# The add passes over VectorE's exponential tiles moved to GpSimd, with other planner quotas

## The chip, the cores and the metric

The kernel runs on one core of a Trainium2 chip. The metric is the device time of one execution in microseconds. Times before: 855.03 and 853.03 us in two runs, median 854.03.

## The reference

The output mixes two branches of one sequence `x` (2048 x 512) with a gate per row. Branch a is full softmax attention with 32 heads of 16 columns, branch b is a convolution whose kernel comes from a diagonal state-space model with 128 states per channel.

```python
x = A_x
g = _sigmoid((x * gate_w).sum(-1, keepdims=True))
a = _A_ref(x, A_wqkv, A_wo)          # scores = q k^T / 4, softmax, times v, times wo
b = _B_ref(x, B_A_re, B_A_im, B_B_re, B_B_im, B_C_re, B_C_im, B_log_dt, B_Dskip)
return g * a + (1 - g) * b
```

## The kernel before

**Attention.** The scores of a block (512 queries of 4 heads) against 128 keys and one head are a tile of 128 x 512. There are 2048 such tiles; three of them make a group, and there are 683 groups, the last of two tiles. TensorE writes a group's scores into one of two PSUM buffers `SC0`, `SC1` (`qk`), then the exponential is taken, and TensorE multiplies the result with the values and adds it up in `OA` (`pv`). As there are two score buffers, the scores of group g+2 cannot be written before group g is read.

**Two engines for the exponential.** ScalarE takes the exponential of a whole group in one instruction (`ex`, line 913, tiles `ET`). In some groups it takes only two of the three tiles and VectorE takes the third (`bits`, line 949): a multiplication and an addition, written as a 16-bit integer, give the bit pattern of a bf16 number near the exponential (tile `DZ`). Four such groups in a row make a set, that is four tiles of the same 128 keys, one for each of the four heads, 128 x 2048 together. To come nearer to the exponential, `batch` adds two constants to the bit patterns (`step`, line 960): 42 gives `DU`, and later 84 gives a new `DZ` in place. TensorE multiplies `DZ`, `DU` and the second `DZ` with the values (`VE`) and with scaled copies of them (`VS`) and adds all three products in `OA`, where the scale corrects each pattern's share. A set thus has four evictions from PSUM, two add passes of 128 x 2048 and 12 products for 4 tiles. Sets have buffers by window of groups: two in groups 180 to 400, two in 400 to 640, three in 640 to 678.

**The other branch.** Beside the attention run the projections, the parameters of the state-space model (VectorE), a table `PT` of powers by block of 32 channels (VectorE, written to `gm_ptd`), from it the states by chunk (`sstage`: TensorE, eviction to `SG`), two scans over 32 chunks (`scan`, half of the channels each, 30 steps of four VectorE operations between two SBUF tensors, lines 1333 to 1340; GpSimd issues one DMA per step, line 1342, out of four buffers `G`), and then 32 y units (`ystage`). Units 0 to 15 need the first scan, 16 to 31 the second. A unit loads `Py` and four pieces of `Tt` (SP's queue, three buffers each), multiplies into the PSUM buffer `MB`, which one user at a time can hold, is evicted as `Yst` (line 1414) and written to DRAM; two units later make a block that SP reads back transposed as `Yl`. When all 16 blocks are back, VectorE adds `Yl` to the attention output of the first three quarters (`AR`), SP loads `Wo`, and TensorE, VectorE and ScalarE finish the last quarter.

**What sets the order.** The program is recorded by a planner (`Sched`) before it runs: each engine gets its instructions in one fixed order, and each waits for what it needs. The planner books a cost for every instruction and takes what its clock says is ready. `decide` chooses the groups of which VectorE takes a tile: a new set begins when VectorE's idle time that is not used up reaches a quota (`dvq`, table `DVQ`, by which stage is already done: `scan1` is the second scan, `scan0` the first, `S15` the last block of states). Idle time saved up is cut at `DVCAP`.

```python
def dvq():
    return next(n for f, n in DVQ if f is None or f in sch.flag)
...
    plan["used"] = max(plan["used"], idle() - DVCAP)
    if plan["set"] is None and clear(x) and idle() - plan["used"] >= dvq():
```

Of the kernel before, what the change touches and what calls it, by code (L numbers as in the profile page):

```python
# [11 lines left out]
ALU = mybir.AluOpType  # L12
# [37 lines left out]
VSP = [len(k) * VSW for k in VKT]  # L50
VSAT = (168, 600)
WIN = ((180, 400, 2, 1), (400, 640, 2, 1), (640, 678, 3, 2))
DVQ = (("scan1", 0.2), ("scan0", 0.8), ("S15", 2.0), (None, 0.7))
BP = 2.2
DVCAP = 2.0
BUP = 1
VW = 136
VG = 4 * VW + 16
# [31 lines left out]
class Prog:  # L90
# [5 lines left out]
    def __init__(self, bufs):  # L96
        self.bufs = bufs
        for b in bufs.values():
            b.st, b.tags, b.closed, b.first, b.last = {}, {}, False, None, None
        self.q = -1  # L100
        self.cap = None
        self.act = 0
        self.cfg = None
        self.busy = 0.0
        self.marg = {}
        self.log = []
        self.tm = {e: 0.0 for e in self.ENG}
        self.fin = {}
        self.ops = {e: [] for e in self.ENG}
        self.cnt = {e: 0 for e in self.ENG}  # L110
        self.known = {e: {} for e in self.ENG}
        self.snap = {}
        self.dn = [0] * (NDSEM + NPSEM)
        self.dnext = self.pnext = 0
        self.need = {e: set() for e in self.ENG}
# [82 lines left out]
    def op(self, eng, fn, R=(), W=(), c=.1, lat=.085, a=0, cfg=None):  # L198
        if self.cap is not None:
            self.cap.append((self.op, (eng, fn, R, W), dict(c=c, lat=lat, a=a, cfg=cfg)))  # L200
            return
        if cfg is not None:
            if cfg != self.cfg:
                c += TURN[cfg]
            self.cfg = cfg
        self.act += a
        self.log.append((self.op, self.q, (eng, fn, R, W)))
        deps = self._deps(eng, R, W)
        i = self.cnt[eng]
        at = self.tm[eng]  # L210
        for s, k in deps.items():
            at = max(at, self.fin[(s, k)] + (.03 if s == eng else .05))
        self.tm[eng] = at + c
        if eng == "DVE":
            self.busy += c
        self.fin[(eng, i)] = at + c + lat
        self.cnt[eng] += 1
        self._record(eng, fn, deps, eng, i, R, W)
        return at + c + lat

    def dma(self, eng, fn, R=(), W=(), c=.45, lat=3.0, m=DMARG):
        if self.cap is not None:
# [393 lines left out]
def record(nc, p, B, ins):  # L616
# [6 lines left out]
    op, dma = p.op, p.dma  # L623
# [331 lines left out]
    def batch(i):  # L955
        z, u, q, b = (sets[i][x] for x in ("z", "u", "q", "b"))
        R = [(z, k, (i, k)) for k in range(4)]

        def step(t, k, W):
            op("DVE", lambda v: v.tensor_scalar(t.u16(0, [[1, 2048]]), z.u16(0, [[1, 2048]]), float(STEP[k][0]), None, ALU.add), R, W, c=.07 + 2048 / 3840)  # L960

        def terms(t, k):
            for n, j in enumerate(sets[i]["js"]):
                pv_mm(4 * q + j, t, 512 * n, [(u, 0, i) if t is u else (z, n, (i, n) if k is None else (i, n, "t"))], QUAD if n == 0 else 0, k)

        yield ("DVE", .6, BUP)
        step(u, 0, [(u, 0, i)])
        yield ("AFTER", f"pv{16 * b}")
        if i:
            yield ("AFTER", f"dvp{i - 1}")  # L970
        yield ("PE", QUAD)
        terms(z, None)
        yield ("AFTER", f"VS{int(q % 16 not in VKT[0])}")
        yield ("PE", QUAD)
        terms(u, 0)
        yield ("DVE", .6, BUP)
        step(z, 1, [(z, k, (i, k, "t")) for k in range(4)])
        yield ("PE", QUAD)
        terms(z, 1)
        sch.mark(f"dvp{i}")  # L980
# [799 lines left out]
```

## Time and profile before

| what | us |
|---|---|
| median of two runs | 854.03 |
| span of the profiled execution | 854.3 |
| ScalarE busy | 826.1 |
| VectorE busy | 766.1 |
| TensorE busy (modelled ends) | 756.7 |
| GpSimd busy | 44.0 |

The profiled execution's own time is its span from the first to the last instruction, 854.3 us, 0.3 above the median of the runs. Busy times of the engines lie beside each other; a row of the group view gives busy time, the mean duration of one, and the idle time ahead of the group with what ended it. Durations of neighbouring instructions on one engine overlap, so that spacing is a better price than the mean duration. In the profile `PE` is TensorE's matmul, `PEld` its weight load, `DVE` VectorE, `ACT` ScalarE, `POOL` GpSimd and `SP` the engine that issues most DMAs; a `q` behind an engine's name is its queue.

### The profile page before, as it was taken

The page shows a single profiled execution, that of the slowest core. Times are in us where ns is not written, and L with a number is a line of the kernel's source. Part 1 is how long each engine was busy: PE and PEld are TensorE (multiplying, and loading weights), DVE is VectorE, ACT ScalarE, POOL GpSimd, SP SyncE. Part 2 cuts the span into 40 slices and gives each one's busy share as a digit, 9 for nine tenths or more (in the row PEclk, how much of TensorE's full clock was granted, in tenths as well). Part 3 has the DMA queues.
Part 4 walks back from the last instruction along what each step waited for, and adds up shares of the span by engine and source line. Part 5 has one row for each costly group of instructions (what it writes and reads, how often), then busy time and mean ns, then how long its engine had stood idle before and what let it go on. Part 6 is the DMA issues. An engine that isn't in the chain of part 4 may idle for free.

```text
span 854.3 us, 23568 instructions
## 1 busy us (share of the span) xinstructions
PE 756.7 (89%) x10301; PEld 296.5 (35%) x10301; DVE 766.1 (90%) x1271; ACT 826.1 (97%) x695; POOL 44.0 (5%) x73
## 2 busy tenths in 40 slices
PE   7888888788768999999999899889988899999986
PEld 3232332222212434343443344334442234443321
DVE  5799999999969988898898999999999978997994
ACT  6999999999979999999999999999999999999996
POOL 4000000000000000000010111101111100000000
PEclk9999999999989999899998999999999999999999
DMA  9400102942933498477394597248998425645120
GB/s 206 118 2 10 35 3 82 194 153 81 73 129 152 51 206 103 149 131 164 62 162 71 84 192 116 36 104 166 199 191 151 120 88 121 136 120 113 25 99 26
DMA packets 218168, 94.55 MB, mean 111 GB/s; under 512 B 185168, under 2 KB 205008, under 8 KB 216016
## 3 DMA queue, kind: packets, MB, share of 16 engines
q1 hardware_dynamic: 207408, 83.99, 45.6%
q0 software_dynamic: 8640, 7.87, 5.9%
q8 instruction: 81, 1.33, 0.6%
q10 hardware_dynamic: 2016, 1.18, 0.6%
q14 instruction: 23, 0.19, 0.1%
HBM read 35.17 MB, written 30.82 MB: 77 GB/s over the span
## 4 chain that ended last, share of the span: by engine, by line
ACT 66%; PE 23%; DMA 5%; DVE 4%; SPq 1%; issue 0%; ACTq 0%; DVEq 0%
ACT ET L913 65%; PE OA L632 9%; PE SC L632 7%; PE MB L632 7%; DMA gm_gd<-g 3%; DMA gm_ytd<-Yst 1%; DMA gm_ptd<-PT 1%; DVE DZ L949 1%; DMA Wq<-in_A_wqkv_dram 1%; DVE s L1333 1%; DVE s L1335 1%; DVE G L1340 0%; DVE s L1338 0%; DVE tt L1007 0%; SPq L1488 0%
## 5 line engine op out<-in xcount | busy, mean ns | idle before, releaser
L913 ACT ACTIVATE ET<-SC 128x1536 bf16<-128x1536 f32 (+1 forms) x683 | 817.8, 1508 | 15.1 <-PE SC L632 13.9
L632 PE MATMUL SC<-Qm,KT 32*128 32x512 bf16 x2048 | 276.5, 387 | 75.9 <-ACT ET L913 61.1
L632 PE MATMUL OA<-wm 128*32 128x256 bf16 (+3 forms) x2193 | 251.6, 341 | 1.2 <-DVE wm L685 1.2
L632 PE MATMUL OA<-ET,VE 128*32 128x512 bf16 x1800 | 181.6, 395 | 4.6 <-DVE OT L984 4.4
L949 DVE TENSOR_SCALAR DZ<-SC 128x512 uint16<-128x512 f32 x248 | 166.2, 685 | 19.1 <-PE SC L632 16.8
L632 PEld LDWEIGHTS SC<-Qm,KT 32*128 32x128 bf16 x2048 | 70.7, 91 | 291.8 <-ACT ET L913 233.9
L632 PEld LDWEIGHTS OA<-wm 128*32 128x32 bf16 (+2 forms) x2193 | 72.9, 95 | 33.8 <-issue 15.5
L632 PEld LDWEIGHTS OA<-ET,VE 128*32 128x32 bf16 x1800 | 46.1, 93 | 106.1 <-issue 98.4
L632 PE MATMUL MB<-X,Qt 64*128 64x32 bf16 x1024 | 74.5, 231 | 0.0
L632 PEld LDWEIGHTS MB<-X,Qt 64*128 64x128 bf16 x1024 | 57.7, 109 | 25.2 <-issue 23.0
L1310 DVE TENSOR_SCALAR SG<-MB 128x512 bf16<-128x512 f32 x64 | 43.9, 686 | 10.6 <-PE MB L632 9.8
L960 DVE TENSOR_SCALAR DZ<-DZ 128x2048 uint16<-128x2048 uint16 x62 | 42.5, 685 | 8.2 <-PE OA L632 8.2
L1342 POOL DMA_DIRECT2D SG<-G x60 | 33.0, 550 | 255.7 <-DVE G L1340 250.9
L1340 DVE TENSOR_TENSOR G<-s,s 128x512 f32<-128x512 f32 x60 | 41.2, 687 | 3.1
L960 DVE TENSOR_SCALAR DU<-DZ 128x2048 uint16<-128x2048 uint16 x62 | 42.3, 685 | 0.4
L1333 DVE TENSOR_TENSOR s<-G,MU 128x512 f32<-128x512 f32 x60 | 41.2, 687 | 1.0
L1338 DVE TENSOR_TENSOR s<-s,SG 128x512 f32<-128x512 f32 x60 | 41.1, 685 | 0.0
L1335 DVE TENSOR_TENSOR s<-G,MU 128x512 f32<-128x512 f32 x60 | 41.0, 683 | 0.0
L1007 DVE TENSOR_TENSOR ft<-FP,L 128x1024 f32<-128x1024 f32 (+1 forms) x32 | 34.4, 1084 | 0.1
L1007 DVE TENSOR_TENSOR PT<-tt,tt 128x1024 bf16<-128x1024 bf16 x48 | 32.8, 683 | 0.4
L632 PEld LDWEIGHTS MB<-Py,SG 128*32 128x32 bf16 x1024 | 29.6, 165 | 8.2 <-issue 4.1
L984 DVE STREAM_TRANSPOSE OT<-OA 128x512 f32<-128x512 f32 x32 | 22.8, 712 | 9.2 <-PE OA L632 8.8
(166 smaller groups left out, 625.6 us busy)
## 6 DMA issues: line engine op xcount, KB each, us to landing
gm_ptd<-PT SPq DMA_DIRECT2D x16, 1024.0 KB, 6.1
Py<-gm_ptd SPq DMA_DIRECT2D x32, 512.0 KB, 5.0
SG<-G POOLq DMA_DIRECT2D x60, 128.0 KB, 3.1
gm_kpd<-Kst SPq DMA_DIRECT2D x16, 256.0 KB, 3.5
Tt<-gm_kpd SPq DMA_DIRECT2D x128, 32.0 KB, 3.5
gm_xrd<-in_A_x_dram SPq DMA_DIRECT2D x1, 2048.0 KB, 13.2
X<-gm_xrd SPq DMA_DIRECT2D x8, 256.0 KB, 5.0
Wo<-in_A_wo_dram SPq DMA_DIRECT2D x4, 512.0 KB, 4.4
```

The source lines that it names most:

```text
L632: op("PE", lambda t: t.matmul(out(), lhsT(), rhs(), start=start, stop=stop, skip_group_check=True, **kw), R, W, c=c, lat=.15, a=a, cfg=cfg)
L913: op("ACT", lambda a: a.activation(ET(512 * e, [[1, 512 * n]]), sc(0, [[1, 512 * n]]), AF.Exp, scale=DH ** -0.5), [(sc, i, g) for i in ran ...
L949: op("DVE", lambda v: v.tensor_scalar(z.u16(512 * k, [[1, 512 * n]]), sc(512 * na, [[1, 512 * n]]), XS, XB, ALU.mult, ALU.add), [(sc, na + ...
L960: op("DVE", lambda v: v.tensor_scalar(t.u16(0, [[1, 2048]]), z.u16(0, [[1, 2048]]), float(STEP[k][0]), None, ALU.add), R, W, c=.07 + 2048 ...
L984: op("DVE", lambda v: v.transpose(OT(512 * w, [[1, 512]]), OA(0, [[1, 512]])), [(OA, 0, b)], [(OT, w, b)], c=.64)
L1007: op(eng, lambda v: v.tensor_tensor(o(), a(), b_(), f), R, W, c=c)
L1310: op("DVE", lambda v, bank=bank, par=par, part=part: v.tensor_scalar(sg(2 * SGH + SGH * part + CB * k8 + 16 * par, [[2 * SGH, 32], [1, 16] ...
L1333: op("DVE", lambda v, g0=g0: v.tensor_tensor(s2(0, W), g0(0, W), MU(d0, [[0, 2], [1, 256]]), ALU.mult), [(g0, 0)] + key("MU"), [(s2, 0)], ...
L1335: op("DVE", lambda v, g0=g0: v.tensor_tensor(s3(0, W), g0(256, [[-256, 2], [1, 256]]), MU(D + d0, [[D, 2], [1, 256]]), ALU.mult), [(g0, 0) ...
L1338: op("DVE", lambda v, so=so: v.tensor_tensor(s2(0, W), s2(0, W), sg(so, W), ALU.add), [(s2, 0)] + ks, [(s2, 0)], c=F5)
L1340: op("DVE", lambda v, g1=g1: v.tensor_tensor(g1(0, [[1, 512]]), s2(0, [[1, 512]]), s3(0, [[1, 512]]), ALU.add), [(s2, 0), (s3, 0)], [(g1, ...
L1342: later("POOL", .3, 0, lambda so=so, g1=g1, c=c: dma("POOL", lambda e: e.dma_start(sg(so, [[1, 512]]), g1(0, [[1, 512]])), [(g1, 0)], [(sg ...
```

## The change

The two passes of `step` are issued on GpSimd instead of VectorE, and the plan books 2.2 us for one (`PSH`) instead of 0.6. The quota that holds before any of these stages is done rises from 0.7 to 1.5, and the cap on saved idle time goes from 2.0 to 1.0. The planner also learns that passes on GpSimd and those VectorE operations that read no PSUM exclude each other (`port`): the one that comes second is booked to start when the first is through.

```diff
-DVQ = (("scan1", 0.2), ("scan0", 0.8), ("S15", 2.0), (None, 0.7))
+DVQ = (("scan1", 0.2), ("scan0", 0.8), ("S15", 2.0), (None, 1.5))
 BP = 2.2
-DVCAP = 2.0
+PSH = 2.2
+DVCAP = 1.0
...
+        if eng == "POOL" and R and fn is not None and W[0][0].name[:2] in ("DZ", "DU") or eng == "DVE" and not any(b.kind == "ps" for b, *_ in R):
+            at = self.port(eng, at, c)
...
+    def port(self, eng, at, c):
+        o = "DVE" if eng == "POOL" else "POOL"
+        for lo, hi in self.held[o][-12:]:
+            if lo <= at < hi:
+                at = hi
+                if eng == "DVE" and self.tm[o] > hi:
+                    self.tm[o] += c
+                break
+        self.held[eng].append((at, at + c))
+        return at
...
-            op("DVE", lambda v: v.tensor_scalar(t.u16(0, [[1, 2048]]), z.u16(0, [[1, 2048]]), float(STEP[k][0]), None, ALU.add), R, W, c=.07 + 2048 / 3840)
+            op("POOL", lambda v: v.tensor_scalar(t.u16(0, [[1, 2048]]), z.u16(0, [[1, 2048]]), float(STEP[k][0]), None, ALU.add), R, W, c=PSH)
...
-        yield ("DVE", .6, BUP)
+        yield ("POOL", PSH, BUP)
         step(u, 0, [(u, 0, i)])
```

With the cap at 1.0, quotas of 1.5 and 2.0 cannot be reached; a set can begin only once the first scan is through. The two programs compare as follows, by the order of their instructions:

| | before | after |
|---|---|---|
| sets | 62 | 49 |
| first set begins in group | 182 | 353 |
| sets that begin in groups 180 to 339, 340 to 519, 520 to 678 | 20, 12, 30 | 0, 24, 25 |
| exponentials of three, of two tiles | 434, 249 | 486, 197 |
| add passes on VectorE, on GpSimd | 124, 0 | 0, 98 |
| score group at which y units 0, 16 and 31 begin | 426, 533, 639 | 361, 641, behind the last |

Up to group 184 the instructions of all five engines are the same.

On TensorE this is the end of the program before, from the last score product (`SC<-Qm,KT`) on; `OA<-wm` and `MB<-wm` are products with zeros.

```order
L632 MATMUL SC<-Qm,KT 128x512 x2
L632 MATMUL OA<-wm 32x512 x12
L632 MATMUL OA<-ET,VE 32x512 x4
L632 MATMUL OA<-wm 32x512 x4
L632 MATMUL MB<-Yl,idb 128x512
L632 MATMUL MB<-Wo,OnT_74 128x512 x3
L632 MATMUL SC<-Yl,idb 128x512
```

And this is TensorE in the changed program, from the last score product on.

```order
L647 MATMUL SC<-Qm,KT 128x512 x2
L647 MATMUL MB<-Py,SG_170 32x64 x16
L647 MATMUL MB<-Tt,XY_182 32x64 x8
L647 MATMUL OA<-wm 32x512 x4
L647 MATMUL OA<-wm 32x256 x4
L647 MATMUL OA<-ET,VE 32x512 x4
L647 MATMUL MB<-Tt,XY_182 32x64 x8
L647 MATMUL OA<-wm 32x512 x4
L647 MATMUL MB<-wm 32x256 x4
L647 MATMUL MB<-Py,SG_170 32x64 x24
L647 MATMUL OA<-DZ_65,VS_55 32x512 x4
```

Half of a y unit and then the products of eleven whole units (`MB<-wm` x4, `MB<-Py` x32, `MB<-Tt` x16) have come between the last score product and `MB<-Yl,idb`.

On SP's queue this is the end of the y units before, up to the loads and writes of the outputs.

```order
L1432 DMA_TRANSPOSE Yl<-gm_ytd 128x16x32
L1359 DMA Py<-gm_ptd 128x2x1024
L1419 DMA gm_ytd<-Yst 128x4x64
L1365 DMA Tt<-gm_kpd 64x4x64 x4
L1419 DMA gm_ytd<-Yst 128x4x64
L1432 DMA_TRANSPOSE Yl<-gm_ytd 128x16x32
L1419 DMA gm_ytd<-Yst 128x4x64
L741 DMA Qm<-gm_qd 16x512 x4
L1419 DMA gm_ytd<-Yst 128x4x64
L1432 DMA_TRANSPOSE Yl<-gm_ytd 128x16x32
L1546 DMA out_dram<-AR_76 128x4x512
L636 DMA Wo<-in_A_wo_dram 128x4x512
```

The same place in the changed program:

```order
L1374 DMA Py<-gm_ptd 128x2x1024
L1447 DMA_TRANSPOSE Yl<-gm_ytd 128x16x32
L1434 DMA gm_ytd<-Yst 128x4x64
L1380 DMA Tt<-gm_kpd 64x4x64 x3
L1434 DMA gm_ytd<-Yst 128x4x64
L1380 DMA Tt<-gm_kpd 64x4x64
L1374 DMA Py<-gm_ptd 128x2x1024
L1380 DMA Tt<-gm_kpd 64x4x64 x4
L1447 DMA_TRANSPOSE Yl<-gm_ytd 128x16x32
L1434 DMA gm_ytd<-Yst 128x4x64 x2
L1447 DMA_TRANSPOSE Yl<-gm_ytd 128x16x32
L1561 DMA out_dram<-AR_76 128x4x512
```

The loads of queries for later blocks (`Qm<-gm_qd`) are no longer among the last units' loads and writes: they stand ahead of them, and the units' DMAs follow each other closely.

On VectorE this is a place among the early sets before, with the states' evictions (`SG<-MB`) beside them.

```order
L960 TENSOR_SCALAR DZ_59<-DZ_59 128x2048
L1310 TENSOR_SCALAR SG_169<-MB 128x32x16
L949 TENSOR_SCALAR DZ_57<-SC 128x512 x3
L1310 TENSOR_SCALAR SG_169<-MB 128x32x16
L949 TENSOR_SCALAR DZ_57<-SC 128x512
L949 TENSOR_SCALAR DZ_59<-SC 128x512
L960 TENSOR_SCALAR DU_58<-DZ_57 128x2048
```

In the changed program sets stand only behind the first scan; this is a place in the second scan (`s` and `G` are its operations).

```order
L1350 TENSOR_TENSOR s_176<-G_172,MU 128x512
L1353 TENSOR_TENSOR s_175<-s_175,SG_170 128x512
L1429 TENSOR_TENSOR Yst<-MB,gt 128x256
L964 TENSOR_SCALAR DZ_63<-SC 128x512
L1355 TENSOR_TENSOR G_173<-s_175,s_176 128x512
L964 TENSOR_SCALAR DZ_63<-SC 128x512 x3
L1348 TENSOR_TENSOR s_175<-G_173,MU 128x512
L1350 TENSOR_TENSOR s_176<-G_173,MU 128x512
L964 TENSOR_SCALAR DZ_61<-SC 128x512
```

The passes of line 960 are gone from VectorE, and the second scan's operations stand among the evictions of sets. The second scan ended behind 32 of 62 sets before, and now ends behind 39 of 49.

More of the change, by code (lines that the diff above doesn't have):

```diff
@@ L105, in __init__ @@
         self.marg = {}
+        self.held = {"DVE": [], "POOL": []}
         self.log = []
@@ L975, in batch @@
         terms(u, 0)
-        yield ("DVE", .6, BUP)
+        yield ("POOL", PSH, BUP)
         step(z, 1, [(z, k, (i, k, "t")) for k in range(4)])
```

## The prediction

> **What bounds the kernel now.** I read the page's busy times and chain first, then ScalarE's order of time, then ScalarE's groups by form.
>
> ```profile
> span 854.3 us, 23568 instructions
> PE 756.7 (89%) x10301; PEld 296.5 (35%) x10301; DVE 766.1 (90%) x1271; ACT 826.1 (97%) x695; POOL 44.0 (5%) x73
> ACT 66%; PE 23%; DMA 5%; DVE 4%; SPq 1%; issue 0%; ACTq 0%; DVEq 0%
> 16.82 194.87 ACT L913 ACTIVATE ET<-SC 128x1536 bf16<-128x1536 f32 x145
> 253.39 1.45 ACT L913 ACTIVATE ET<-SC 128x1536 bf16<-128x1536 f32 x1 [3.99 <-PE SC L632]
> 357.88 16.04 ACT L913 ACTIVATE ET<-SC 128x1024 bf16<-128x1024 f32 x13 [1.10 <-PE SC L632]
> 669.11 175.82 ACT L913 ACTIVATE ET<-SC 128x1536 bf16<-128x1536 f32 x169 [0.37 <-PE SC L632]
> 849.55 0.59 ACT L1742 CAST fo<-MB 128x512 bf16<-128x512 f32 x1 [4.63 <-PE MB L632]
> 255.30:469.00 213.70, 206.11 (x2684) 86.90 (x2680) 193.58 (x320) 206.71 (x178) 5.96 (x11) 0.97 0.64 125
> 469.00:844.90 375.90, 342.30 (x5367) 139.96 (x5367) 341.68 (x562) 374.12 (x330) 28.12 (x51) 1.00 0.56 118
> L913 ACT ACTIVATE ET<-SC 128x1536 bf16<-128x1536 f32 x434 | 593.6, 1713 | 9.7 <-PE SC L632 9.3
> L913 ACT ACTIVATE ET<-SC 128x1024 bf16<-128x1024 f32 x249 | 242.0, 1151 | 5.4 <-PE SC L632 4.7
> ```
>
> The exponentials on ScalarE are the bound: 97% busy, 66% of the chain. In the two window rows (columns: length, then PE, PEld, DVE, ACT, POOL busy) ScalarE is idle for 7.0 us between 255 and 469 us and for 1.8 us from there to its end. The last exponential ends at 669.11 + 175.82 = 844.9, so 9.4 us lie behind it. VectorE at 90% is not the bound, but every tile that it takes is one that ScalarE does not. The mean durations in the group rows overlap, so I price an exponential by spacing: 194.87 / 145 = 1.344 us for three tiles; in the 175.82 us stretch the order has 49 of three and 120 of two, so (175.82 - 49 x 1.344) / 120 = 0.916 for two. A tile more in a group costs 0.43 us of ScalarE.
>
> **Term 1, the tiles given back.** The order has 62 sets before and 49 after, and the count of score groups stays 683; 13 sets x 4 tiles = 52 tiles go back to ScalarE: 52 x 0.43 = +22.2 us. All of it is on the path, since ScalarE waits for nothing else most of the time.
>
> **Term 2, waits that go.** Up to group 184 all five engines have the same order as before, so the 3.99 us wait at 253 stays. Behind it, up to group 353 (at 468 us before), no set is left, and PE has 1.34 us per group instead of 0.92 in the groups that VectorE shared. I take the whole 7.0 us off: the stretch at 16.82 shows 145 groups of three without a wait. Ends: 0 and -8.8.
>
> **Term 3, the passes.** What moves, and the nearest rows for its price:
>
> ```profile
> L949 DVE TENSOR_SCALAR DZ<-SC 128x512 uint16<-128x512 f32 x248 | 166.2, 685 | 19.1 <-PE SC L632 16.8
> L960 DVE TENSOR_SCALAR DZ<-DZ 128x2048 uint16<-128x2048 uint16 x62 | 42.5, 685 | 8.2 <-PE OA L632 8.2
> L960 DVE TENSOR_SCALAR DU<-DZ 128x2048 uint16<-128x2048 uint16 x62 | 42.3, 685 | 0.4
> L1338 DVE TENSOR_TENSOR s<-s,SG 128x512 f32<-128x512 f32 x60 | 41.1, 685 | 0.0
> L632 PE MATMUL SC<-Qm,KT 32*128 32x512 bf16 x2048 | 276.5, 387 | 75.9 <-ACT ET L913 61.1
> L1264 POOL MEMSET Kst<- 128x2048 bf16 x1 | 1.8, 1805 | 0.0
> L1342 POOL DMA_DIRECT2D SG<-G x60 | 33.0, 550 | 255.7 <-DVE G L1340 250.9
> ```
>
> VectorE loses 124 passes (84.8 us) and 52 tile evictions (52 x 0.685 = 35.6 us), and none of that is worth anything by itself. GpSimd gains 2 x 49 = 98 passes. The trace has no such pass; the nearest row is a memset that writes the same 2048 elements in 1.805 us, the lower end. A pass that read and wrote one after the other would take twice that, 3.6 us, the upper end (an estimate). The plan books 2.2, and the order was made with that number: PE's products with DU and DZ stand where a 2.2 us pass would be done, with nothing in reserve. I take 1.8 to 2.2, nearest to the memset, so the length alone costs nothing.
>
> What costs is that VectorE's and GpSimd's queues now run at the same tiles. The first scan is through before the first set, but all 30 steps of the second (4 operations of 0.685 us each) now stand between the evictions of sets, 41 of which begin before group 640. An eviction has some slack: its two score tiles must be free two groups on, so 2 x 0.916 less one product (0.387) and the eviction (0.685) = 0.76 us. A scan operation held for a whole pass uses that up and leaves about 1.4 us to ScalarE. I expect this in one set of four, and as much again for PE waiting at a product: 41 x 0.25 x 1.4 = 14, in all about +15 us. Ends: 0 (no two operations hinder each other) and +60 (both in every set that precedes the second half of the y units). The scan's DMA issues, 0.55 us each, now queue behind passes on GpSimd; four G buffers cover a delay of three steps, so I cost this at nothing as long as a pass is below some 4 us.
>
> By the Trainium skill, page "SBUF — State Buffer", section "Who interferes with whom", GpSimd shares a port pair with VectorE, an operation of VectorE with two SBUF inputs contends with GpSimd reads, and the one that comes second is blocked until the first ends. No run here shows it yet: in this trace only DMA issues of GpSimd meet the scan, and its operations hold 0.685. By that rule the waits of this term exist and by its absence they are 0, so the sum would be 941 or 926.
>
> **Term 4, what now stands behind the last exponential.** The plan delays the second scan (its last step stands behind 39 of 49 sets; before, behind 32 of 62), and the y units of the second half start at score group 641 instead of 533. Before, unit 31 stood at group 639. Now half of unit 20 and all of units 21 to 31 stand behind the last score product, so they cannot begin until ScalarE is two groups from its end. What a unit needs:
>
> ```profile
> 599.91 0.57 SPq L1359 DMA_DIRECT2D Py<-gm_ptd  x1
> 600.58 1.26 SPq L1365 DMA_DIRECT2D Tt<-gm_kpd  x2
> 601.89 0.65 SPq L1419 DMA_DIRECT2D gm_ytd<-Yst  x1
> 602.59 1.23 SPq L1365 DMA_DIRECT2D Tt<-gm_kpd  x2
> 805.82 1.23 SPq L1432 DMA_TRANSPOSE Yl<-gm_ytd  x1
> Py<-gm_ptd SPq DMA_DIRECT2D x32, 512.0 KB, 5.0
> Tt<-gm_kpd SPq DMA_DIRECT2D x128, 32.0 KB, 3.5
> gm_ytd<-Yst SPq DMA_DIRECT2D x32, 64.0 KB, 3.6
> Yl<-gm_ytd SPq DMA_TRANSPOSE x16, 2.8
> Wo<-in_A_wo_dram SPq DMA_DIRECT2D x4, 512.0 KB, 4.4
> 615.06 0.58 PE L632 MATMUL MB<-Py,SG 128*32 128x64 bf16 x24
> 616.53 0.27 PE L632 MATMUL MB<-Py,SG 128*32 128x64 bf16 x8
> 616.73 0.31 PE L632 MATMUL MB<-Tt,XY 64*32 64x64 bf16 x8
> L1414 DVE TENSOR_TENSOR Yst<-MB,gt 128x256 bf16<-128x256 f32 x32 | 13.4, 418 | 2.2 <-PE MB L632 1.5 <-DMA gm_ytd<-Yst 0.7
> 812.51 6.69 DVE L1544 TENSOR_TENSOR AR<-AR,Yl 128x2048 bf16<-128x2048 bf16 x3
> 844.85 0.81 PE L632 MATMUL MB<-Wo,OnT 128*128 128x512 bf16 x3
> 846.91 0.72 DVE L984 STREAM_TRANSPOSE OT<-OA 128x512 f32<-128x512 f32 x1 [6.46 <-PE OA L632]
> ```
>
> PE and VectorE need 0.58 + 0.27 + 2 x 0.31 + 0.42 = 1.9 us per unit, 2.2 with hand-overs, but Py and Tt have three buffers, so the loads of unit u wait for unit u-3, and SP issues them: 0.67 for Py, 4 x 0.65 for Tt, 0.70 for the write of Yst, 1.27 for a transposed read every second unit. Behind unit 21's eviction SP has 8 Py, 32 Tt, 10 writes and 6 reads left: 5.4 + 20.8 + 7 + 7.6 = 41 us. Stepped through in SP's order, with loads landing 5.0 and 3.5 us after issue, writes 3.6 and reads 2.8, unit 31 is evicted 41 to 42 us after unit 21 and the last Yl lands 48 us after it. Unit 21 itself is evicted about 1.6 us behind the last exponential (last score product 2.2 us before its end, half a unit and one unit behind that).
>
> Then the end: the first AR sum (2.3), its DMA issue (0.4), and behind it on SP the load of Wo, 4.4, which before lay under the exponentials; 0.1 for a semaphore: 7.2 us. The three AR sums (6.7) lie beside it. From the first Wo product to OT took 2.06 us (844.85 to 846.91), and from OT to the end 7.4. Together 1.6 + 48 + 7.2 + 2.06 + 7.4 = 66 us where 9.4 stood: +56.6. Ends: with SP's issue free the ring and the landings alone give 40.5 instead of 48, so +49; with landings 1 us slower 52.4, and 2 us for the end, so +63. What hid all this before were the exponentials; that cover is gone for 11 of 32 units.
>
> **The sum.** 854.3 + 22.2 - 7.0 + 15 + 56.6 = 941. The span is the time here: the runs' median is 854.03, 0.3 below it, which I neglect.
>
> **The rivals.**
> A: the passes take well over the booked 2.2 us, or VectorE's operations keep GpSimd out so long that they end late; in either case the 85 us taken off VectorE come back as waits, and the change does not do what it says. PE waits in order at each DU and DZ product, and ScalarE behind it. At 3.6 us each pass is 1.4 late, 98 x 1.4 = 137 us if all shows: 1063 in place of the 15 us. For it: no margin in the order. Against: the memset row. Chance 0.15. The Trainium skill, page "GPSIMD Engine Reference", section "Engine selection", calls operations with one input roughly line-rate, which speaks against A.
> B: nothing hinders anything; ScalarE has no waits behind 255 us and SP issues ahead: 854.3 + 22.2 - 8.8 + 49 = 917, up to 926 with SP's pace. For it: the scan row's 0.685 beside GpSimd's DMAs. Against: two engines that had not met. Chance 0.2.
> C, the other side: the y units behind the last score product cost nothing extra, because PE runs far enough ahead of ScalarE to get them done under it. Then only 854.3 + 22.2 - 8.8 = 867.7 remains, 1.6% above. It decides if less than 13 us lie behind the last exponential instead of 66. Against: the two score buffers let PE be at most two groups (2.2 us) ahead. Chance 0.03.
>
> **How the numbers follow.** The forecast has 0.6, A 0.15, B 0.2, C 0.03, and 0.02 is for anything else. The time is the forecast's, 941. The forecast's ends are 917 (which B shares) and 854.3 + 22.2 - 7.0 + 60 + 63 = 992; this leaves out most of A, and C. About 2% is what a measurement of this kernel can tell from no change: 837 to 871. Below it lies none of the cases (0.01 for what I cannot see), within it C (0.03), above it all else (0.96).
>
> **What would show it.** ScalarE's exponentials should be 486 of three tiles and 197 of two, and end at about 875 us; from 255 us to group 353 ScalarE should show no wait. About 66 us should lie behind the last exponential, with SP issuing Py and Tt one after the other and PE mostly idle, 4 us per y unit. A GpSimd pass should read 1.8 to 2.2 us. Waits of ScalarE for PE should sum to about 15 us in the stage with sets, with VectorE's scan operations longer than 0.69 or started late. The forecast is wrong if passes of 3 us or more appear, if ScalarE idles over 60 us ahead of its last exponential, or if fewer than 30 us lie behind it.

## The result, and the profile after

The changed kernel takes 1171.68 us (median of two runs, 1170.56 to 1172.8) against 854.03: 1.371 times as long, 95% interval 1.365 to 1.377. The prediction was 941, with a range to 992. It had the direction, and it missed by 231 us.

The page of the changed kernel: span, busy times, the chain by engine, and the 40 slices (29.3 us each) of GpSimd and of TensorE's clock.

```profile
span 1171.0 us, 24477 instructions
PE 877.8 (75%) x10774; PEld 314.1 (27%) x10803; DVE 807.0 (69%) x1095; ACT 865.8 (74%) x695; POOL 575.9 (49%) x171
POOL 3000000000000011179679899999889889999700
PEclk8999999989999999978677756778677676666656
POOL 35%; ACT 24%; PE 21%; issue 7%; DVE 6%; DMA 4%; SPq 3%; POOLq 0%; ACTq 0%; DVEq 0%
```

ScalarE fell from 97% busy to 74% and from 66% of the chain to 24%. GpSimd's 49% is a mean over stages with different limits: but for the first, its slices read 0 or 1 up to about 500 us, and 8 or 9 in most of those from there to 1110 us. The number of that stage counts, and there GpSimd is the bound. TensorE's granted clock falls in the same slices, to a mean of 0.819 over the span; the same order with shorter passes (512 columns, below) shows 0.952, so the lower clock goes along with the waits for the passes.

ScalarE's order of time, start and length first, the wait ahead of a row in brackets:

```profile
254.55 1.45 ACT L928 ACTIVATE ET<-SC 128x1536 bf16<-128x1536 f32 x1 [3.84 <-PE SC L647]
256.62 248.25 ACT L928 ACTIVATE ET<-SC 128x1536 bf16<-128x1536 f32 x182 [0.61 <-PE SC L647]
1091.66 1.02 ACT L928 ACTIVATE ET<-SC 128x1024 bf16<-128x1024 f32 x1 [4.01 <-PE SC L647]
1166.01 0.59 ACT L1757 CAST fo<-MB 128x512 bf16<-128x512 f32 x1 [73.33 <-PE MB L647]
```

Up to 505 us all is as forecast: one stretch of 182 exponentials without a wait of note. The last exponential then ends at 1092.7 instead of the forecast 875, and 78.3 us lie behind it instead of 66. Nearly all of the miss lies between 505 and 1093 us, the stage with sets.

The window of most of that stage (length; PE, PEld, DVE, ACT, POOL busy; clock, DMA share, GB/s):

```profile
505.00:1041.00 536.00, 377.97 (x4169) 106.83 (x4176) 359.40 (x358) 346.15 (x300) 485.46 (x117) 0.71 0.19 43
```

Of 536 us ScalarE works 346 and VectorE 359; GpSimd works 485. Between the start of its first pass and the end of its last (504.7 to 1106.9 us) it is busy 549 of 602 us. Its groups, and the group of the products behind its passes (busy, mean ns | idle before, and what ended it):

```profile
L975 POOL TENSOR_SCALAR DU<-DZ 128x2048 uint16<-128x2048 uint16 x49 | 269.1, 5494 | 30.6 <-DVE DZ L964 30.3
L975 POOL TENSOR_SCALAR DZ<-DZ 128x2048 uint16<-128x2048 uint16 x49 | 264.4, 5397 | 27.3 <-PE OA L647 25.6
L647 PE MATMUL OA<-DZ,VS 128*32 128x512 bf16 x196 | 27.2, 545 | 133.9 <-POOL DZ L975 133.9
```

A pass takes 5.4 us. The plan booked 2.2 and the prediction took 1.8 to 2.2. Ninety-eight of them make 533.5 us. The waits show how that reaches ScalarE (total, times, longest):

```profile
ACT ET L928 <- PE SC L647: 194.5, 141, 10.1
PE OA L647 <- POOL DZ L975: 133.9, 38, 9.2
PE OA L647 <- POOL DU L975: 26.0, 13, 4.3
```

TensorE works in order. It stands 160 us at products whose DZ or DU tile GpSimd has not finished, the score products queue behind them, and ScalarE waits 194.5 us for those.

### The profile page after: what moved, and what is told of

Its sections match the earlier page's. It is cut to its first block, busy times and chain, and to the rows that moved or that the text cites. A ratio compares the mean times of both kernels' runs of the same rounds, so it can differ in the third digit from the quotient of the medians.

```text
span 1171.0 us, 24477 instructions
## 1 busy us (share of the span) xinstructions
PE 877.8 (75%) x10774; PEld 314.1 (27%) x10803; DVE 807.0 (69%) x1095; ACT 865.8 (74%) x695; POOL 575.9 (49%) x171
## 4 chain that ended last, share of the span: by engine, by line
POOL 35%; ACT 24%; PE 21%; issue 7%; DVE 6%; DMA 4%; SPq 3%; POOLq 0%; ACTq 0%; DVEq 0%
ACT ET L928 24%; POOL DZ L975 18%; POOL DU L975 16%; PE OA L647 9%; PE SC L647 6%; PE MB L647 6%; DMA gm_gd<-g 2%; DVE DZ L964 2%; SPq L1380 1%; DVE s L1350 1%; DMA gm_ptd<-PT 1%; DVE s L1348 1%; DMA Wq<-in_A_wqkv_dram 1%; DVE s L1353 1%; POOL SG L1357 0%
## 5 line engine op out<-in xcount | busy, mean ns | idle before, releaser
L928 ACT ACTIVATE ET<-SC 128x1536 bf16<-128x1536 f32 (+1 forms) x683 | 857.5, 1461 | 223.6 <-PE SC L647 194.5
L647 PE MATMUL SC<-Qm,KT 32*128 32x512 bf16 x2048 | 312.6, 440 | 72.7 <-ACT ET L928 52.1
L647 PE MATMUL OA<-wm 128*32 128x512 bf16 (+3 forms) x2735 | 316.6, 379 | 1.2 <-DVE wm L700 1.2
L975 POOL TENSOR_SCALAR DU<-DZ 128x2048 uint16<-128x2048 uint16 x49 | 269.1, 5494 | 30.6 <-DVE DZ L964 30.3
L975 POOL TENSOR_SCALAR DZ<-DZ 128x2048 uint16<-128x2048 uint16 x49 | 264.4, 5397 | 27.3 <-PE OA L647 25.6
L964 DVE TENSOR_SCALAR DZ<-SC 128x512 uint16<-128x512 f32 x196 | 131.4, 684 | 167.5 <-PE SC L647 167.1
L647 PE MATMUL OA<-DZ,VS 128*32 128x512 bf16 x196 | 27.2, 545 | 133.9 <-POOL DZ L975 133.9
L1355 DVE TENSOR_TENSOR G<-s,s 128x512 f32<-128x512 f32 x60 | 79.0, 1316 | 2.4
L1348 DVE TENSOR_TENSOR s<-G,MU 128x512 f32<-128x512 f32 x60 | 76.4, 1273 | 1.1
L1350 DVE TENSOR_TENSOR s<-G,MU 128x512 f32<-128x512 f32 x60 | 76.9, 1282 | 0.0
L1353 DVE TENSOR_TENSOR s<-s,SG 128x512 f32<-128x512 f32 x60 | 67.2, 1119 | 0.0
```

The costliest lines, as they stand in the source:

```text
L647: op("PE", lambda t: t.matmul(out(), lhsT(), rhs(), start=start, stop=stop, skip_group_check=True, **kw), R, W, c=c, lat=.15, a=a, cfg=cfg)
L928: op("ACT", lambda a: a.activation(ET(512 * e, [[1, 512 * n]]), sc(0, [[1, 512 * n]]), AF.Exp, scale=DH ** -0.5), [(sc, i, g) for i in ran ...
L964: op("DVE", lambda v: v.tensor_scalar(z.u16(512 * k, [[1, 512 * n]]), sc(512 * na, [[1, 512 * n]]), XS, XB, ALU.mult, ALU.add), [(sc, na + ...
L975: op("POOL", lambda v: v.tensor_scalar(t.u16(0, [[1, 2048]]), z.u16(0, [[1, 2048]]), float(STEP[k][0]), None, ALU.add), R, W, c=PSH)
L1348: op("DVE", lambda v, g0=g0: v.tensor_tensor(s2(0, W), g0(0, W), MU(d0, [[0, 2], [1, 256]]), ALU.mult), [(g0, 0)] + key("MU"), [(s2, 0)], ...
L1350: op("DVE", lambda v, g0=g0: v.tensor_tensor(s3(0, W), g0(256, [[-256, 2], [1, 256]]), MU(D + d0, [[D, 2], [1, 256]]), ALU.mult), [(g0, 0) ...
```

## The experiments

Each run stands against the kernel before on the same chip, where that took 855.6 to 857.4 us (medians); ratios are therefore safer than differences. Where the passes are written anew, line numbers shift by a few.

### The pass shortened: 512, 1024 and 1536 columns

The order and waits are the change's; the products of the columns that are left out read the tile as evicted.

```diff
-    op("POOL", lambda v: v.tensor_scalar(t.u16(0, [[1, 2048]]), z.u16(0, [[1, 2048]]), float(STEP[k][0]), None, ALU.add), R, W, c=PSH)
+    op("POOL", lambda v: v.tensor_scalar(t.u16(0, [[1, 512]]), z.u16(0, [[1, 512]]), float(STEP[k][0]), None, ALU.add), R, W, c=PSH)
...
-    pv_mm(4 * q + j, t, 512 * n, ...)
+    pv_mm(4 * q + j, z if 512 * n >= 512 else t, 512 * n, ...)
```

> The changed kernel with each add pass on GpSimd cut to the first 512 of its 2048 columns; the products that would use the other columns take the pattern without the constant, so the last three quarters of each set's correction are left out. Planned costs, order, waits and buffers are those of the changed kernel. Theory L (the pass is 5.4 us long where the order was made for 2.2, and nothing else is wrong): a pass of some 1.4 us is always done in time, ScalarE's waits behind group 353 fall from over 200 us to under 30, and the time is that of the order alone, 915 to 945 us, with about 65 us behind the last exponential. Rival P (it is the sharing of SBUF between GpSimd and VectorE, whatever the pass's length): scan operations stay stretched to several us and the time stays above 1050. Rival Q (the new quotas and the order that they make are at fault): about 1150.

> The same with 1024 of 2048 columns; the last half of each set's correction is left out. By the slope of the full pass (2.6 ns per column) a pass takes 2.7 us, 0.5 above the booked 2.2. Theory L: some waits show, at most 98 x 0.5 = 49 us more than with 512 columns, so 930 to 990 us. Rival P: above 1080. Rival Q: about 1150.

> The changed kernel with its 98 passes cut to the first 1536 of 2048 columns (the products of the last 512 read the uncorrected pattern), the order and the waits being the changed kernel's. A pass should take 4.07 us (2.6 ns a column as between 1024 and 2048). Theory S (GpSimd is full: 98 passes and the 60 shifts it issues need longer than the exponentials, so time follows the length of the work on GpSimd): 98 x 1.30 = 127 us less than the changed kernel, 1045 us, GpSimd busy over 90 per cent between the first and the last pass, and hardly any gain below 3.6 us a pass, which agrees with 961 at 2.77 us and 951 at 1.48. Rival B (GpSimd is not the limit; the two passes in a row at each end of a block, about 11 us at full length, hold TensorE): 9 ends of a block, 2.6 us less at each, 25 us less than the changed kernel, 1140 to 1150.

Measured: 951.31 us (ratio 1.110, 1.106 to 1.115), 961.29 us (1.122, 1.117 to 1.127) and 1078.13 us (1.259, 1.256 to 1.262). With 512 columns, the passes (ns: min, median, max) and ScalarE's end:

```profile
L975 POOL TENSOR_SCALAR DZ<-DZ x49: 1477/1488/1831, 507.5 to 875.9; 128x512 uint16<-128x512 uint16 x49
```

```profile
837.75 36.51 ACT L928 ACTIVATE ET<-SC 128x1024 bf16<-128x1024 f32 x35 [0.82 <-PE SC L647]
942.21 0.58 ACT L1757 CAST fo<-MB 128x512 bf16<-128x512 f32 x1 [67.95 <-PE MB L647]
```

The exponentials end at 874.3 us (forecast: 875), and 73.2 us lie behind them (forecast: 66). With passes shorter than booked, the prediction's sum is met to about 10 us. With 512 columns the time is 6 us above theory L's 945, with 1024 it lies within its 930 to 990; rivals P and Q (1050 and more) are out.

The last pass of GpSimd with 1024 columns, then with 1536, then at full length:

```profile
889.56 2.77 POOL L975 TENSOR_SCALAR DZ<-DZ 128x1024 uint16<-128x1024 uint16 x1 [0.77 <-PE OA L647]
```

```profile
1008.26 4.09 POOL L975 TENSOR_SCALAR DZ<-DZ 128x1536 uint16<-128x1536 uint16 x1 [1.20 <-PE OA L647]
```

```profile
1101.55 5.38 POOL L975 TENSOR_SCALAR DZ<-DZ 128x2048 uint16<-128x2048 uint16 x1 [1.20 <-PE OA L647]
```

The passes begin at 504 to 507 us in all three and end at 892.3, 1012.4 and 1106.9. Behind them lie 69.1, 64.0 and 64.1 us, so the time follows the end of GpSimd's work. Per pass that stretch is 3.96, 5.15 and 6.15 us, 0.7 to 1.2 us above the pass's own length. The exponentials need 874 - 505 = 369 us for the same sets, 3.8 us for each pass. So the knee should lie near 2.8 us (an estimate): below it a shorter pass gains little (10 us from 1024 to 512 columns), above it most of its length counts (117 of 129 us from 1024 to 1536 columns). From 1536 to 2048 columns 93.5 us were added where 127 were expected; GpSimd idles 22 us less ahead of its passes at full length (57.9 instead of 79.8). Rival B (1140 or more) is out, but theory S holds only in the main: 1078 is 33 us above its 1045, and GpSimd is busy 426 of 505 us between its first and last pass, 84% and not over 90. What fills the rest was not taken apart; the waits at the ends of blocks (below) may be part of it.

### The quotas alone

The passes stay on VectorE, booked at 0.6 us; quotas and cap are those of the change. With them the planner forms 51 sets, not 49, none of them before group 353.

```diff
-    op("POOL", lambda v: v.tensor_scalar(...), R, W, c=PSH)
+    op("DVE", lambda v: v.tensor_scalar(...), R, W, c=.07 + 2048 / 3840)
```

> The changed kernel's quotas and cap, with the passes on VectorE and booked at 0.6 us as before. The order has 51 sets (62 before), none before group 353, and all y units done by group 590. Theory L: 11 sets fewer cost 44 tiles x 0.43 = 18.9 us of ScalarE, the 7.0 us of waits before group 353 go, and 9.4 us stand behind the last exponential as before: 862 to 872 us. Rival Q: well above 950, since the quotas alone would make most of the 317 us.

Measured: 874.31 us, ratio 1.020 (1.017 to 1.023), 17 us. The end of ScalarE's order of time:

```profile
784.38 78.86 ACT L928 ACTIVATE ET<-SC 128x1536 bf16<-128x1536 f32 x78 [0.70 <-PE SC L647]
867.86 0.58 ACT L1757 CAST fo<-MB 128x512 bf16<-128x512 f32 x1 [4.62 <-PE MB L647]
```

The exponentials end at 863.2 and 9.4 us lie behind them, as before the change. So the quotas cost 17 us, where 862 to 872 (8 to 18 above 854) was expected, and rival Q is out. The long stretch behind the last exponential belongs to the passes on GpSimd: with the same quotas, the order that was made with their booking has the y units there and this one does not.

### What the operations cost by themselves

A kernel that computes nothing of the reference runs GpSimd's operations alone, then four passes beside 24 operations of VectorE.

> No part of the reference is computed: only passes measured by themselves on GpSimd and VectorE, alone and side by side. Theory L: the add of 2048 uint16 takes 5.4 us on GpSimd with VectorE idle too, 1024 columns 2.7, 512 columns 1.4, in place the same; beside VectorE operations that read PSUM it stays so. Rival P: alone it takes about 2 us and 5.4 only beside VectorE. Open to both: whether bf16 and fp32 passes are faster than uint16 (2.2 us was booked), and how long a VectorE operation with two SBUF inputs, or the pass itself on VectorE, is held beside a pass of GpSimd (up to 4.2 us were seen in the changed kernel).

GpSimd alone (first four passes in order of time, then group rows):

```profile
7.44 21.38 POOL L403 TENSOR_SCALAR UO<-UA 128x2048 uint16<-128x2048 uint16 x4 [7.02 <-DVE TK L392]
L409 POOL TENSOR_SCALAR UO<-UA 128x2048 bf16<-128x2048 bf16 x3 | 16.0, 5365 | 0.2 <-DVE TK L392 0.2
L403 POOL TENSOR_SCALAR UO<-UA 128x1024 uint16<-128x1024 uint16 x4 | 11.0, 2767 | 0.2 <-DVE TK L392 0.2
L412 POOL TENSOR_SCALAR FO<-FA 128x2048 f32<-128x2048 f32 x2 | 10.7, 5362 | 0.2 <-DVE TK L392 0.2
L403 POOL TENSOR_SCALAR UO<-UA 128x512 uint16<-128x512 uint16 x4 | 5.8, 1487 | 0.2 <-DVE TK L392 0.2
L415 POOL TENSOR_TENSOR FO<-FA 128x1024 f32<-128x1024 f32 x2 | 3.7, 1891 | 0.2 <-DVE TK L392 0.2
```

The change's pass takes 21.38 / 4 = 5.35 us with VectorE idle, as theory L said (rival P: about 2 us). 2048 elements take 5.36 us as 16-bit or 32-bit numbers too (a multiplication there): GpSimd's price goes by the element, 2.6 ns each ((5362 - 2767) / 1024 = 2.5 for one more). A two-tensor addition, here with the same tile as both inputs, is cheaper per element (1.89 us for 1024) than this operation with one input (2.77).

Order of time, three kinds of VectorE's operations alone and then side by side with four passes:

```profile
94.08 4.91 DVE L418 TENSOR_TENSOR WO<-FX,FY 128x512 f32<-128x512 f32 x8
99.15 4.91 DVE L421 TENSOR_SCALAR VO<-UA 128x2048 uint16<-128x2048 uint16 x8
104.22 4.88 DVE L424 TENSOR_SCALAR VO<-PS 128x512 uint16<-128x512 f32 x8
...
109.26 28.28 DVE L418 TENSOR_TENSOR WO<-FX,FY 128x512 f32<-128x512 f32 x24
109.31 23.40 POOL L403 TENSOR_SCALAR UO<-UA 128x2048 uint16<-128x2048 uint16 x4 [15.39 <-DVE TK L392]
...
137.70 35.17 DVE L421 TENSOR_SCALAR VO<-UA 128x2048 uint16<-128x2048 uint16 x24
137.75 23.15 POOL L403 TENSOR_SCALAR UO<-UA 128x2048 uint16<-128x2048 uint16 x4 [5.04 <-DVE TK L392]
...
173.04 14.44 DVE L424 TENSOR_SCALAR VO<-PS 128x512 uint16<-128x512 f32 x24
173.09 21.38 POOL L403 TENSOR_SCALAR UO<-UA 128x2048 uint16<-128x2048 uint16 x4 [12.19 <-DVE TK L392]
```

Alone, 24 operations of each kind take 24 x 4.91 / 8 = 14.7 us. Beside four passes the addition of two SBUF tiles (the scan's form) takes 13.6 us more, 3.4 per pass. The 16-bit operation from SBUF to SBUF takes 20.4 more, 5.1 per pass, nearly all of it. The eviction from PSUM is not touched. GpSimd loses 2 us over its four passes beside the first two kinds and nothing beside the third.

### The same passes in a shorter form

Two 16-bit patterns are added as one 32-bit word, as a two-tensor addition with a constant tile, booked at 2.2 us still. All that the change computes is computed, in the change's order on every engine.

```diff
+    op("DVE", lambda v, k=k: v.memset(B["kc"](k, [[1, 1]]), STEP[k][0] * 65537), [], [(B["kc"], 0)], c=.07)
...
-    op("POOL", lambda v: v.tensor_scalar(t.u16(0, [[1, 2048]]), z.u16(0, [[1, 2048]]), float(STEP[k][0]), None, ALU.add), R, W, c=PSH)
+    op("POOL", lambda v: v.tensor_tensor(t(0, [[1, 2048]]).bitcast(INT32), z(0, [[1, 2048]]).bitcast(INT32), kc.add(k), ALU.add), R + [(kc, 0)], W, c=PSH)
```

> The changed kernel with its 98 passes written as another operation of GpSimd: an addition of two 32-bit integer tensors of 1024 elements (two bit patterns to a word; the second operand is one word that holds the constant twice, read with step 0), booked at the same 2.2 us, so that the order of all engines is that of the changed kernel. The result is the same as the change's. Theory L (the time of the change is the pass's own length above what the plan books): the two-tensor addition of 1024 four-byte elements took 1.89 us alone (estimate for integers), below the booked 2.2, so 945 to 960 us, as with the 512-column pass (951.3), and exponentials that end near 875. Rival P (the port held against VectorE's scan operations, whatever the length): some 1.9 us of hold in each of 98 passes, exponentials that end 20 us or more later, 975 or above. If integers go slower than floats (3 us and more), 965 to 1010 by theory L.

Measured: 969.74 us (1.132, 1.128 to 1.136), exponentials until 894.3: 10 us above the upper end of theory L and 19 us later than it said, though short of rival P's 975. Its order of time showed a wait of 16 us where no pass runs yet (first fence); the same kernel with another seed of the search that lays out the buffers, and nothing else changed, shows 3.6 us there (second fence):

```profile
256.69 1.45 ACT L934 ACTIVATE ET<-SC 128x1536 bf16<-128x1536 f32 x1 [16.00 <-PE SC L651]
```

```profile
251.67 1.45 ACT L934 ACTIVATE ET<-SC 128x1536 bf16<-128x1536 f32 x1 [3.61 <-PE SC L651]
949.31 0.58 ACT L1765 CAST fo<-MB 128x512 bf16<-128x512 f32 x1 [68.64 <-PE MB L651]
```

> The kernel with the 32-bit two-tensor addition (969.7 us), all engines in the same order, with another seed of the search that lays out the buffers, so that the scan's table no longer shares an address with the gate's last buffer. Theory A (the address made 12 us of its time): the wait at 255 us falls from 16.0 to about 4 us, the exponentials end at 882 in place of 894, and the time is 955 to 960. Rival: it is the passes, and the time stays at 966 to 973.

Measured: 954.16 us, ratio 1.112 (1.105 to 1.119). Theory A holds, and with it theory L's 945 to 960. In the layout of the 969.7 us kernel one of the tables of powers (`B16`, the last of four, from which `PT` is made) lies over the gate's last buffer `g1`, which a DMA still reads; with the other seed, and in the change, it does not. The exponentials now end at 847.63 + 33.05 = 880.7:

```profile
847.63 33.05 ACT L934 ACTIVATE ET<-SC 128x1536 bf16<-128x1536 f32 x31 [0.34 <-PE SC L651]
```

What the passes cost in this form:

```profile
L983 POOL TENSOR_TENSOR DU<-DZ,kc 128x1024 int32<-128x1024 int32 x49 | 103.9, 2120 | 103.9 <-DVE DZ L970 103.9
L983 POOL TENSOR_TENSOR DZ<-DZ,kc 128x1024 int32<-128x1024 int32 x49 | 97.2, 1984 | 50.2 <-PE OA L651 49.2
```

At 2.05 us a pass, close to what was booked, the change costs 96 us (0.112 x 856.7) instead of 318.

### Passes that nobody waits for

Both products of a set read the evicted tile and the correction is left out. GpSimd works one pass per set, of 2048 or of 64 columns, in a tile that nobody else reads.

```diff
+COLS = 2048   # 64 in the control
+    op("POOL", lambda v: v.tensor_scalar(u.u16(0, [[1, COLS]]), u.u16(0, [[1, COLS]]), 42.0, None, ALU.add), [(u, 0)], [(u, 0)], c=PSH)
-    terms(u, 0)
-    step(z, 1, ...)
-    terms(z, 1)
+    terms(z, None)
+    terms(z, None)
```

> What do GpSimd's passes cost when nobody waits for them? The kernel leaves the correction out: both products of a set read the uncorrected pattern, and GpSimd works one pass of 2048 columns per set on a tile that nobody else reads (59 sets here, booked at 5.4 us, so that GpSimd keeps up). Beside it runs the same order with a pass of 64 columns; the difference of the two is all that the passes do to other engines. Theory L: none of it lies on the path; within 10 us of the 64-column kernel, both near 965 us (20 y units of 4 us behind the last exponential). Rival P: in the changed kernel VectorE's scan operations took some 135 us longer in all (299.5 us against 240 x 0.69), 1.4 us for each of 98 passes; 59 passes then hold VectorE by 60 to 80 us, and if that lies on the path the kernel is 40 to 80 us above the 64-column one, with its exponentials ending later by as much.

> The control of the pass that nobody reads: the same order and bookings, with 64 columns in place of 2048, so that GpSimd is idle for nearly all of that time. The correction is left out as there. Both theories: exponentials that end near 860 us (59 sets, 10 more than in the changed kernel, 4 tiles of 0.43 us each), a tail of some 105 us, 965 us; scan operations of 0.69 us.

Measured: 1057.9 us (1.236, 1.231 to 1.242) and 1018.21 us (1.189, 1.185 to 1.194): 40 us apart. One scan operation in each, with the long pass and with the short one:

```profile
L1349 DVE TENSOR_TENSOR s<-G,MU 128x512 f32<-128x512 f32 x60 | 67.6, 1126 | 1.0
```

```profile
L1349 DVE TENSOR_TENSOR s<-G,MU 128x512 f32<-128x512 f32 x60 | 41.2, 687 | 1.0
```

VectorE is busy 768.8 us in the one and 691.0 in the other, 78 us more for 59 passes, and the exponentials end 33.8 us later (920.7 against 886.9). So my theory L was wrong here: the passes hold VectorE, and about half of that reaches the path, 0.7 us a pass, the lower end of rival P's 40 to 80 us. Even the kernel with the short pass lies 53 us above its forecast of 965: 129 us instead of 105 stand behind its last exponential, and its exponentials end at 887 instead of 860.

### The pass booked at its real length

```diff
-PSH = 2.2
+PSH = 5.4
```

> The changed kernel with the pass booked at what it takes (5.4 us in place of 2.2), so that the plan forms 38 sets in place of 49 and 76 passes in place of 98. Theory L: 76 x 5.37 = 408 us of GpSimd work in some 370 us behind group 353, or just in step with it: the exponentials wait little (0 to 40 us), end at 875 + 11 x 4 x 0.43 = 894 to 930, and with 70 us behind them the time is 955 to 1005; 170 us or more of the 220 between the changed kernel and the 512-column one go. Rival P: each pass costs others 1.4 us and more, whatever is booked; 76 of them leave at least 105 us of the loss, 1060 or above.

Measured: 1090.07 us (1.272, 1.266 to 1.278). Theory L gave at most 1005 and exponentials that end by 930, and they end at 1023; it fails here, and the number would fit rival P. ScalarE's waits named a third cause:

```profile
ACT ET L928 <- PE OA L647: 100.3, 13, 19.5
```

In order of time three of them that follow one another:

```profile
651.15 2.37 ACT L928 ACTIVATE ET<-SC 128x1536 bf16<-128x1536 f32 x2 [8.61 <-PE OA L647]
...
687.76 2.48 ACT L928 ACTIVATE ET<-SC 128x1536 bf16<-128x1536 f32 x2 [8.62 <-PE OA L647]
...
724.40 1.45 ACT L928 ACTIVATE ET<-SC 128x1536 bf16<-128x1536 f32 x1 [10.11 <-PE OA L647]
```

Waits of about 9 us stand 37 us apart, as do the blocks of 16 key tiles there. A set that is formed last in its block needs two passes one after the other, 11 us, before the block can be closed, whatever is booked. The next kernel forms no set late in a block:

```diff
-LEFT = 3
+LEFT = 9
-WIN = (..., (640, 678, 3, 2))
+WIN = (..., (640, 678, 2, 2))
```

> The kernel with the pass booked at 5.4 us (1090 us, in which ScalarE waits 100 us in 13 waits of about 10 us, one at the end of each block of 16 key tiles), and no set of VectorE tiles begun when 9 key tiles or fewer are left in its block (3 before), with two sets of buffers in place of three at the end. 31 sets and 62 passes; 16 y units behind the last exponential, as in the changed kernel. Theory B (the two passes in a row of a set that is formed at the end of a block hold TensorE, and it the exponentials): the waits for the products fall from 100 us to below 30, and with 40 us of other waits (the port) the exponentials end at 875 + 18 x 4 x 0.43 + 40 to 70 = 945 to 975; with 75 us behind them 1020 to 1050. Rival P (it is each pass's hold on VectorE that ends in these waits): they fall only with the number of passes, 100 x 62 / 76 = 80 us, and the time stays at 1070 to 1100.

Measured: 1058.72 us (1.237, 1.234 to 1.241).

```profile
ACT ET L928 <- PE OA L647: 32.1, 19, 7.2
1051.13 0.59 ACT L1757 CAST fo<-MB 128x512 bf16<-128x512 f32 x1 [94.11 <-PE MB L647]
```

The waits fell to 32 us (theory B: below 30, rival P: 80), and the exponentials end at 957.0, 66 us earlier than with the 38 sets, though ScalarE has 28 tiles more. The late sets, the third set of buffers and 7 sets in all went together, so their shares are not separated. The time is above the forecast (1020 to 1050), as 99 us stand behind the last exponential instead of 75: 16 y units and not the eleven and a half of the changed kernel, from which I had taken the 75.

### The passes moved late only

The quotas and cap of before; passes on VectorE until both scans are done, then on GpSimd in the 32-bit form, booked at 1.95 us. The order has 62 sets, as before (the expectation's 63 was a slip).

```diff
+late = lambda: "scan1" in sch.flag
+if not late():
+    op("DVE", lambda v: v.tensor_scalar(...), R, W, c=.07 + 2048 / 3840)
+    return
```

> Whether a move of the passes can pay at all: the kernel before with its quotas; the passes stay on VectorE until both scans are done, and from there on (60 passes) go to GpSimd as the two-tensor addition of 32-bit words, 2.06 us in place of 0.60. VectorE gets 36 us of room where no scan runs, but sets are formed there every four groups, as close as the plan can, with it or without (63 sets against 62). Theory: what sets the end there is ScalarE, so 850 to 862 us, no change. Rival: VectorE is late there in the kernel before, and the room shows: 845 or less. Second rival: the longer pass at the ends of blocks holds TensorE, 3 us at each of some six ends, 870 or more.

> The late move alone (880.6 us) with the other seed. Theory A: the wait at 255 us falls from 15.7 to about 4 us, 867 to 871 us; what is left, some 13 us over the kernel before, is the cost of the late move itself (8 us more of waits for score products, 2 us of exponentials). Rival: the late move costs nothing, and 850 to 862 us are left; second rival: no change, 878 or more.

Measured: 880.62 us (1.029, 1.026 to 1.031), above the theory's 862, with the same 16 us wait by the address: VectorE's first write to that table waits for the DMA from the gate's buffer.

```profile
DVE B L1036 <- DMA gm_gd<-g: 17.2, 1, 17.2
```

With the other seed it takes 865.69 us (1.011, 1.006 to 1.016), just below theory A's 867 to 871 and above the 862 of its first rival. So even short passes, where no scan is left to hold, seem to cost some 9 us rather than nothing; that is within the 2% that count as no change, and part of it may be the other layout, which the kernel before did not get. Waits of the exponentials for score products in this kernel, then in the kernel before:

```profile
ACT ET L935 <- PE SC L652: 19.8, 34, 4.4
```

```profile
ACT ET L913 <- PE SC L632: 13.9, 26, 4.0
```

So 6 of the 9 us can be seen there. I have not separated them further. No kernel of this study beats the one before.

## Why the prediction was wrong

**The step that failed is in term 3: "I take 1.8 to 2.2, nearest to the memset, so the length alone costs nothing."** The pass takes 5.37 us. The memset of 2048 elements was the wrong neighbour: it reads nothing and adds nothing, and which of the two makes the difference is not shown; the upper end, 3.6 us for a pass that reads and writes one after the other, was built on the same row and was also too low. Even that end gave only 1063 (rival A), so no range made from these bounds could hold the time. The Trainium skill's page "GPSIMD Engine Reference", section "Engine selection", which calls one-input operations roughly line-rate, was read as evidence against rival A; the runs differ from it (2.6 ns an element), and the measurement decides.

**Rival A had the right mechanism.** Products wait in order for the pass (160 us), and ScalarE behind them (194.5 us). Two of the prediction's three signs of being wrong are there: passes of 3 us or more, and ScalarE idle for over 60 us. Rival A's price, the excess over the booking times 98, would have been 98 x (5.37 - 2.2) = 311 us. Measured is 0.259 x 855 = 221 us between the 32-bit form and the change. It is less because not every excess shows. What decides in the main is that GpSimd's work (6.1 us a pass with what lies between) fills 602 us where the exponentials need 369, 233 us more.

**The waits of term 3 (+15).** With the length taken out (the 32-bit form) the exponentials end 5.6 us later than forecast, after 25 us of waits in the whole kernel, 21 of them behind the one at 252 us. The term was right in kind and small against the length. The hold itself is shown by the passes that nobody reads. In the changed kernel, a scan operation, then the pass beside it:

```profile
516.48 4.23 DVE L1353 TENSOR_TENSOR s<-s,SG 128x512 f32<-128x512 f32 x1
```

```profile
516.51 5.38 POOL L975 TENSOR_SCALAR DU<-DZ 128x2048 uint16<-128x2048 uint16 x1
```

The operation begins with the pass, and ends 1.2 us ahead of it instead of after 0.69 us. The Trainium skill's page "SBUF — State Buffer", section "Who interferes with whom", states which forms meet (two inputs from SBUF do, one from PSUM does not), and the runs agree. It says that the first holds the shared ports for its whole instruction, and says this of VectorE's two-port modes; here the 16-bit form is held for 5.1 of 5.37 us, the scan's form for 3.4. The delay of the scan's DMA issues was taken at nothing "as long as a pass is below some 4 us". That condition fell with the length, but the delay still shows no cost: ahead of the operations that write the buffers `G`, VectorE idles 2.4 us in all (3.1 before).

**Terms 1 and 2 (+22.2 and -7.0) were right.** There are 486 and 197 exponentials as said, and no wait of note from 255 to 505 us. The quotas alone, with 51 sets, cost 17 us, where the two terms give 44 x 0.43 - 7.0 = 11.9 for that order: right to some 5 us.

**Term 4 (66 us behind the last exponential) was right in kind and 7 us short.** It is 73.2 with 512 columns, 73.4 in the 32-bit form. In the former the evictions of units 21 to 31 span 47 us (876.7 to 923.9) instead of 41 to 42, which makes most of the difference. In the changed kernel 78.3 us stand there, where GpSimd's last passes still run for 14 us after the last exponential.

**In sum:** of the 317 us, about 17 are the quotas, 79 the y units pushed behind the exponentials and the waits at passes near the booked length (1.112 less 1.020), and 221 the length beyond that. The shares are rough, as the run with the quotas alone has two sets more. The first two are what the prediction had reckoned with: 1.112 times 854 is 950, where it said 941.

## What to carry to other kernels

An operation that has no row in the trace is not priced by a row of another kind on the same engine: a write alone says little of a read, a computation and a write. If such a price decides the sign or the size, the range must reach to the time at which that engine becomes the bound; here one line would have given it: 98 passes in 369 us bear 3.8 us each, all else included.

Before work is moved to an idle engine, look at its length, at the chain that it lengthens (with two passes in a row at the ends of blocks, ScalarE waited 100 us even when they were booked right), and at what it holds on the engine it was taken from.

## What was not expected of the hardware

- GpSimd's operation with a scalar takes 2.6 ns an element in 16-bit and 32-bit types (5.36 us for 2048), while its addition of two tensors takes 1.85 ns (1.89 us for 1024, the same tile read twice): the form with more inputs is the cheaper one, and packing two 16-bit numbers into a word halves the count besides, 5.37 to 2.05 us a pass in the kernel.
- A pass holds VectorE's operations by their form: 5.1 us for a 16-bit operation from SBUF to SBUF, 3.4 us for an addition of two SBUF tiles, nothing for an eviction from PSUM.
- Two words more in SBUF gave a wait some 12 us longer in two kernels, by an address shared with a buffer still in use; with another seed of the layout search it went, and the times fell from 969.7 to 954.2 us and from 880.6 to 865.7.
